# Regrouping an attention tile's TensorE work beside a two-layer expert network

## The chip, the cores and the metric

The kernel runs on one core of one Trainium2 chip. The metric is the device time of one launch in microseconds. TensorE does all matrix products; VectorE (DVE), ScalarE (ACT) and GpSimd (POOL) do the elementwise work; SyncE (SP) issues the DMAs. Each engine works through its own list of instructions in order and waits where an input is not ready.

## The reference, cut to what matters

An mLSTM with exponential gates (4 batch rows, 8 heads, 768 steps, head size 40), then two expert layers on 3072 tokens of width 320 with 2048 hidden units.

```python
for t in range(S):                                   # per batch row and head
    m_new = maximum(f[t] + m, i[t])
    f_stab, i_stab, m = exp(f[t] + m - m_new), exp(i[t] - m_new), m_new
    C = f_stab * C + i_stab * outer(v[t], k[t])      # 40 x 40 state
    n = f_stab * n + i_stab * k[t]
    y[t] = sigmoid(o[t]) * (C @ q[t]) / maximum(abs(n @ q[t]), 1.0)
x = y as [3072, 320]
x = square(maximum(x @ w_in, 0)) @ w_out             # first layer
h = x @ w2_in
out = (h * sigmoid(h)) @ w2_out                      # second layer
```

## The kernel before, in words

The recurrence is worked in chunks of 128 steps: 24 tiles of 128 tokens (`TILES`, a batch row and a chunk each; tiles 0 to 17 interleave three batch rows, 18 to 23 are the fourth). For one tile the steps are, by the names in the plan:

- `q`, `v`, `w`, `e`: loads; `sk`, `sj`: queries and keys split into float32r parts and stacked by DMA (`stk`); `m0`, `m1`, `x0`, `x1`: the decay weights W of the two halves of four heads.
- `s0`, `s1` (`SC`, L479): scores of heads 0 to 3 and 4 to 7, four products each, every half into a psum bank. `d0`, `d1` (`SD`): VectorE multiplies them by W and splits the result into three bf16 parts.
- `vk` (`VK`, L521): VectorE (in a few tiles GpSimd) scales the keys in place, for the state.
- `h` (`HG`, L547 and L558): head outputs, in groups of three, three and two heads. A group is one float32 product of the query with the state of the chunk before (L547, two instructions in the trace; none in the first chunk of a batch row), then six bf16 value products for each head (L558). Tiles 3 to 5 have float32 value products (L553) instead.
- `ev` (`EV`): VectorE divides and gates hA and makes y. `st` (`ST`, L585): the state products of the chunk, from vk, six instructions; none in the last chunk of a batch row. `gr`, `gm` (`GR`, `GM`): VectorE adds them into the state cc and masks it (in the first chunk ScalarE copies them out, L595 and L596).
- `xt` (`XT`, L618): three transposes of y. `xa`, `xl`: ScalarE and VectorE copy them out as the first layer's input x.

Scores, hA, state and transposes take their banks from one psum pool, `p_at`, with three banks.

The first layer runs in eight blocks of 384 tokens, three tiles each. In a block, a slot j of 16 has eight products for the hidden units three slots ahead (L677, `hin`) and eight for the output (L732 to L739, `o`). Tiles of the next blocks are worked between them: `base(i)` gives the slot at which tile i begins (16/3 slots per tile, six slots ahead), and `plan(i)` adds an offset for each step. Up to slot 16 (`KF`, block 0) a step's place comes from a written order with due times (`ORDER`); from there on steps are put into half slots by `at_slot` and issued by `run_events` in order of their time, first after the slot's `hin` products, then after its `o` products. In the blocks from the second to the last but one, TensorE, ScalarE, VectorE and SyncE keep exactly the order in which the program issues; in block 0 GpSimd does too. From the last block on only TensorE does. Tiles from 8 on begin at slot 16 or later, tile 7 at 15.33. The second layer (L749 to L751) has no attention beside it.

In steady state the steps of one tile on TensorE were so placed, in slots from its base b:

```python
("s0", b, ...), ("s1", b + 1.0, ...), ("vk", b + 2.6, VK),      # vk: VectorE
("h", b + 3.3, ...), ("ev", b + 3.9, EV), ("st", b + 4.4, ST),  # ev: VectorE
("xt", min(b + 6.1, e - 1.6), XT)                               # e: the block's due slot
```

The next tile's base is b + 5.33, so `xt` stood about 0.77 slot after the next tile's `s0`.

Of the kernel before, what the change touches and what calls it, by code (L numbers as in the profile page):

```python
# [18 lines left out]
PAIRS = ((2, 0), (1, 0), (1, 1), (0, 2), (0, 1), (0, 0))  # L19

B, H, S, D = 4, 8, 768, 40
# [3 lines left out]
NTILE = NT // L  # L25
KF = DFF // 128
# [11 lines left out]
N_EARLY = 3  # L38
# [76 lines left out]
def top(ap):  # L115
    return ap.bitcast(BF16).rearrange("p (n two) -> p n two", two=2)[:, :, 1]
# [3 lines left out]
def mlstm_moe_kernel(  # L120
# [14 lines left out]
    pe, act, dve, pool, sp = nc.tensor, nc.scalar, nc.vector, nc.gpsimd, nc.sync  # L135
# [185 lines left out]
    T = {}  # L321
# [135 lines left out]
    def sc_bank(i, hf):  # L457
        if i == 0:
            return p_in.tile([128, 512], F32, tag="in", name="sc")
        if i == 1:  # L460
            return p_out.tile([128, 512], F32, tag=f"o{1 + hf}", name="sc")
        return p_at.tile([128, 512], F32, tag="at", name="sc")

    def SC(i, hf):
        d = T[i]
        if i < N_NAT:
            if hf == 0:
                for p in range(2):
                    d["sc", p] = sc_bank(i, p)
                for h in range(4):  # L470
                    for p in range(2):
                        x = d["kq"][64 * p:64 * p + D]
                        pe.matmul(d["sc", p][:, h * L:(h + 1) * L], x[:, 0, h], x[:, 1, h], start=True, stop=True)
            return
        ps = d["sc", hf] = sc_bank(i, hf)
        for h in range(4):
            g, x = divmod(4 * hf + h, 3)
            gs = slice(g * L, (g + 1) * L)
            pe.matmul(ps[:, h * L:(h + 1) * L], d["stk"][0:120, x, 0, gs], d["stk"][0:120, x, 1, gs],  # L479
                      start=True, stop=True)  # L480

    def SD(i, hf):
        d = T[i]
        ps = d["sc", hf]
        w = d["W", hf]
        if i < N_EARLY:
            dve.tensor_tensor(out=w, in0=ps.rearrange("p (h t) -> p h t", h=4), in1=w, op=ALU.mult)
            d["p1", hf] = w.rearrange("p h t -> p (h t)")
            return
        if i < N_NAT:  # L490
            p = d["p1", hf] = at.tile([128, 4 * L], F32, tag="pr", name="pn", bufs=2)
            dve.tensor_tensor(out=p, in0=ps, in1=w.rearrange("p h t -> p (h t)"), op=ALU.mult)
            return
        dve.tensor_tensor(out=w, in0=ps.rearrange("p (h t) -> p h t", h=4), in1=w, op=ALU.mult)
        w = w.rearrange("p h t -> p (h t)")
        d["p1", hf] = top(w)
        r = at.tile([128, 4 * L], F32, tag="pr", name="pr", bufs=2)
        d["p2", hf] = top(r)
        p3 = d["p3", hf] = at.tile([128, 4 * L], BF16, tag="p3", name="p3", bufs=2)
        on(f"pr{hf}", i).tensor_tensor(out=r, in0=w, in1=d["p1", hf], op=ALU.subtract)  # L500
        on(f"p3{hf}", i).tensor_tensor(out=p3, in0=r, in1=d["p2", hf], op=ALU.subtract)
# [30 lines left out]
        q = d["q"][0:120].rearrange("p (g t) -> p g t", g=3)  # L532
        (pool if PLAN.get(f"@qt{i}", i < N_NAT) else dve).tensor_tensor(out=q, in0=q, in1=eqv(i)[0:120], op=ALU.mult)

    def HG(i, g):
        d = T[i]
        n = min(3, H - 3 * g)
        b, c = TILES[i]
        if g == 0 and i < N_EARLY:
            d["hA"] = p_out.tile([128, 512], F32, tag=f"o{i}", name="hA")  # L540
        elif g == 0:
            d["hA"] = p_at.tile([128, 512], F32, tag="at", name="hA")
        ov = d["hA"][:, 0:VW].rearrange("p (h c) -> p h c", c=42)
        if c:
            k = 40 * n
            q = d["q"][0:k, g * L:(g + 1) * L]
            pe.matmul(ov[:, 3 * g:3 * g + n], q, T["cm", b % 3][0:k, 3 * g:3 * g + n], start=True, stop=False)  # L547
        if i < N_NAT:
            v = d["vk"][:, DM:DM + VW].rearrange("p (h c) -> p h c", c=42)
            for h in (range(4 * g, 4 * g + 4) if i < N_EARLY else range(3 * g, 3 * g + n)):  # L550
                hf, k = place(i, h)
                p = d["p1", hf][:, k * L:(k + 1) * L]
                pe.matmul(ov[:, h], p, v[:, h], start=c == 0, stop=c == 0 or h == 3 * g + n - 1)  # L553
            return
        for h in range(3 * g, 3 * g + n):
            ps = [d[x, h // 4][:, (h % 4) * L:(h % 4 + 1) * L] for x in ("p1", "p2", "p3")]
            for m, (x, y) in enumerate(PAIRS):
                pe.matmul(ov[:, h], ps[x], d["v"][y][:, h], start=c == 0 and m == 0, stop=m == len(PAIRS) - 1 and (c == 0 or h == 3 * g + n - 1))  # L558

    def EV(i):  # L560
        d = T[i]
# [73 lines left out]
    i = 0  # L635
# [145 lines left out]
    if True:  # L781
# [29 lines left out]
        def base(i):  # L811
            if i < 2 * nb0:
                return 0.3 + 3.3 * (i - nb0)
            return KF * (i // 3 - 1) + KF * (i % 3) / 3 - EV_AHEAD

        def plan(i):
            b = base(i)
            p = base(i - 2) if i >= nb0 + 2 else -20.0
            e = KF * (i // 3) - AHEAD
            q0, v0, w0, e0 = b - 8.0, b - 5.0, b - 6.4, b - 4.6  # L820
            if i < nb0 + 2:
                q0, v0, w0, e0 = [(t - F0) / SLOT for t in LOADS[i - nb0]]
            else:
                q0, v0 = max(q0, p + (1.2 if i < N_NAT else 2.4)), max(v0, p + 4.8)
                w0, e0 = max(w0, p + 3.8), max(e0, p + 5.5)
            todo = [("q", q0, load_q), ("v", v0, load_v), ("w", w0, load_w), ("e", e0, load_e),
                    ("sk", max(b - 4.9, q0 + 0.6), SK), ("sj", max(b - 4.2, q0 + 1.2), SK2),
                    ("m0", b - 2.4, lambda i: WT(i, 0)), ("m1", b - 2.3, lambda i: WT(i, 1)),
                    ("x0", b - 1.8, lambda i: WE(i, 0)), ("x1", b - 1.2, lambda i: WE(i, 1)), ("vv", b - 1.5, VV),
                    ("s0", b, lambda i: SC(i, 0)), ("d0", b + 0.5, lambda i: SD(i, 0)), ("qt", b + 0.9, QT),  # L830
                    ("s1", b + 1.0, lambda i: SC(i, 1)), ("d1", b + 1.5, lambda i: SD(i, 1)),
                    ("vk", b + 2.6, VK),
                    ("h", b + 3.3, lambda i: (HG(i, 0), HG(i, 1), HG(i, 2))), ("ev", b + 3.9, EV),
                    ("st", b + 4.4, ST), ("gr", b + 4.9, GR), ("gm", b + 4.91, GM),
                    ("xt", min(b + 6.1, e - 1.6), XT), ("xa", min(b + 6.6, e - 1.1), XA),
                    ("xl", min(b + 6.9, e - 0.6), XL)]
            if i % 3 == 0:
                todo.append(("sg", b - 0.9, lambda i: load_s(i // 3)))
                todo.append(("si", b + 1.5, lambda i: sig(i // 3)))
            need = {"sk": "q", "sj": "sk", "m0": "w", "m1": "w", "x0": "m0", "x1": "m1", "s0": "q sj", "s1": "s0", "d0": "s0 x0",  # L840
                    "d1": "s1 x1", "qt": "q e", "vv": "v", "vk": "v", "h": "d0 d1 vv v qt", "ev": "h", "st": "vk vv v h", "gr": "st e",
                    "gm": "gr", "xt": "ev", "xa": "xt", "xl": "xa", "si": "sg", "e": "gd", "w": "gd", "x": "aw"}
            for nm, x, fn in todo:
                if x < KF or f"{nm}:{i}" in PLAN:
                    after = [f"{y}:{i}" for y in need.get(nm, "").split() if y not in ("gd",)]
                    if nm in ("w", "e"):
                        after += ["gD1", "eD1"]
                    if nm in ("m0", "x0", "vk"):
                        after += ["take"]
                    if nm in ("sk", "sj") and i < N_NAT:  # L850
                        continue
                    if nm == "h" and TILES[i][1]:
                        after.append(f"gm:{i - 3}")
                    if nm == "gr" and TILES[i][1]:
                        after += [f"gr:{i - 3}", f"h:{i}"]
                    if nm == "gm" and TILES[i][1]:
                        after += [f"h:{i}"]
                    if nm == "ev":
                        after.append(f"si:{i // 3 * 3}")
                    after = [y for y in after if y != f"sj:{i}" or i >= N_NAT]  # L860
                    GUESS[f"{nm}:{i}"] = F0 + SLOT * x
                    add(f"{nm}:{i}", lambda fn=fn: fn(i), *after)
                else:
                    at_slot(x, lambda fn=fn: fn(i))
# [21 lines left out]
        for k, (n, tag) in enumerate(WARM):  # L886
            n = int(PLAN.get(f"#warm{k}", n))
# [49 lines left out]
        for k, e in enumerate(wq):  # L937
            dec = []
            b = base(6 + k)
# [155 lines left out]
```

## Time and profile before

| | |
|---|---|
| median of 3 runs | 850.65 us (849.47 to 863.62) |
| profiled execution, its own time | 850.39 us |
| span of that execution in the trace | 848.7 us |
| TensorE busy | 824.7 us, 97% of the span |
| VectorE, ScalarE, GpSimd busy | 505.6, 492.5, 85.7 us |
| granted TensorE clock, mean | 0.994 |

The span runs from the first to the last instruction of the program on the core; 1.7 us of the time lie outside it. In the rows, L is a line of the kernel before; `out<-in` are the program's names; a form such as 120x126 is partitions x elements. The ends of matmuls are modelled and overlap the next one's start, so lengths of TensorE work are read from the chain of waits, where pieces follow one another without overlap.

### The profile page before, as it was taken

The numbers are of one execution on the slowest core, as the hardware profiler recorded it, in microseconds if no ns is written. First come the engines' busy times: TensorE is split into PE (matmuls) and PEld (weight loads), VectorE is DVE, ScalarE is ACT, GpSimd is POOL, SyncE is SP. The second block draws the span as 40 slices with busy tenths as digits, with TensorE's granted clock in tenths as the row PEclk, the third lists the DMA queues.
The fourth block names the chain that finished last, engine by engine and source line by source line (L and its number), as shares of the span: only waits on it lengthen the run. The fifth ranks groups of instructions, "written<-read, shape, count | busy, mean of one in ns | idle before, by whom it ended". The sixth has DMA issues, their size and how long they took to land.

```text
span 848.7 us, 14676 instructions
## 1 busy us (share of the span) xinstructions
PE 824.7 (97%) x5569; PEld 773.4 (91%) x5569; DVE 505.6 (60%) x905; ACT 492.5 (58%) x966; POOL 85.7 (10%) x110
## 2 busy tenths in 40 slices
PE   7888899999999999999999999999999999999998
PEld 5677889999999999999999999999999999999997
DVE  3789899888787787787742333353443433433433
ACT  3587787786976977869746553343433433433332
POOL 4244143100001000000000110000000000000000
PEclk9899999999999999999999999999999999999999
DMA  6667758767767676677403990020010000000000
GB/s 234 179 210 245 238 161 269 252 197 237 224 220 238 219 251 219 202 235 229 144 1 119 308 293 31 1 81 1 24 58 1 8 25 0 32 1 1 32 1 32
DMA packets 69014, 115.68 MB, mean 136 GB/s; under 512 B 5175, under 2 KB 47039, under 8 KB 68943
## 3 DMA queue, kind: packets, MB, share of 16 engines
q1 hardware_dynamic: 68943, 114.74, 42.8%
q8 instruction: 44, 0.72, 0.4%
q14 instruction: 27, 0.22, 0.1%
HBM read 75.48 MB, written 19.33 MB: 112 GB/s over the span
## 4 chain that ended last, share of the span: by engine, by line
PE 87%; DVE 2%; DMA 2%; ACT 1%; SPq 1%; issue 1%; POOL 1%; DVEq 0%; POOLq 0%; ACTq 0%
PE hin L677 40%; PE o L751 7%; PE o L750 7%; PE o L749 7%; PE o L732 5%; PE o L733 5%; PE o L734 5%; PE hA L558 3%; PE o L737 2%; PE o L739 2%; PE hA L547 2%; PE sc L479 2%; PE st L585 1%; DMA rqk<-in_qk_dram 1%; DMA W<-g_d 1%; DMA wo<-w2o_d 1%
## 5 line engine op out<-in xcount | busy, mean ns | idle before, releaser
L677 PE MATMUL hin<-x,wi 128*128 128x384 f32 (+1 forms) x1792 | 400.1, 365 | 5.9 <-ACT r L687 2.9
L677 PEld LDWEIGHTS hin<-x,wi 128*128 128x128 f32 x1792 | 321.7, 189 | 33.8 <-ACT r L687 3.7
L708 DVE TENSOR_TENSOR gl<-r,gh 128x384 fp32r<-128x384 f32 (+1 forms) x224 | 140.8, 631 | 112.4 <-ACT gh L694 60.7
L694 ACT ACTIVATE gh<-r 128x384 fp32r<-128x384 f32 (+1 forms) x224 | 127.8, 571 | 70.9 <-DVE r L690 65.4
L690 DVE TENSOR_TENSOR r<-hin,r 128x512 f32<-128x512 f32 x96 | 66.4, 691 | 136.4 <-ACT r L689 136.4
L689 ACT ACTIVATE r<-hin 128x512 f32<-128x512 f32 x96 | 57.3, 597 | 148.2 <-PE hin L677 148.2
L751 PE MATMUL o<-wo,gl 128*128 128x320 f32 x384 | 118.7, 309 | 0.0
L750 PE MATMUL o<-wo,gh 128*128 128x320 f32 x384 | 118.5, 309 | 0.0
L749 PE MATMUL o<-wo,gh 128*128 128x320 f32 x384 | 118.2, 308 | 0.0
L687 ACT ACTIVATE r<-hin 128x384 f32<-128x384 f32 x128 | 62.1, 487 | 84.0 <-PE hin L677 80.5
L732 PE MATMUL o<-gh,wo 128*128 128x384 f32 x256 | 89.6, 350 | 0.0
L734 PE MATMUL o<-gl,wo 128*128 128x384 f32 x256 | 86.7, 339 | 1.3 <-DVE gl L708 1.3
L733 PE MATMUL o<-gh,wo 128*128 128x384 f32 x256 | 86.8, 339 | 0.1
L749 PEld LDWEIGHTS o<-wo,gh 128*128 128x128 f32 x384 | 72.1, 188 | 3.6
L750 PEld LDWEIGHTS o<-wo,gh 128*128 128x128 f32 x384 | 72.1, 188 | 3.6
L751 PEld LDWEIGHTS o<-wo,gl 128*128 128x128 f32 x384 | 72.1, 188 | 0.0
L702 ACT ACTIVATE r<-r 128x384 f32<-128x384 f32 x123 | 64.6, 525 | 3.9
L444 POOL TENSOR_SCALAR_AFFINE_SELECT W<-W 128x512 f32<-128x512 f32 x42 | 32.8, 804 | 246.9 <-DMA W<-g_d 176.5
L455 ACT ACTIVATE W<-W,aw 128x128 f32<-128x128 f32 x168 | 52.9, 390 | 0.1
L734 PEld LDWEIGHTS o<-gl,wo 128*128 128x128 f32 x256 | 48.3, 189 | 1.7 <-DVE gl L708 1.7
L733 PEld LDWEIGHTS o<-gh,wo 128*128 128x128 f32 x256 | 48.4, 189 | 0.6 <-POOL wo L296 0.5
L732 PEld LDWEIGHTS o<-gh,wo 128*128 128x128 f32 x256 | 48.5, 189 | 0.4
(142 smaller groups left out, 1015.6 us busy)
## 6 DMA issues: line engine op xcount, KB each, us to landing
stk<-tt SPq DMA_DIRECT2D x162, 120.0 KB
raw<-in_w_in_dram SPq DMA_DIRECT2D x16, 768.0 KB
W<-g_d SPq DMA_DIRECT2D x21, 512.0 KB
raw<-in_w_out_dram SPq DMA_DIRECT2D x16, 640.0 KB
vk<-in_vk_dram SPq DMA_DIRECT2D x23, 328.0 KB
rqk<-in_qk_dram SPq DMA_DIRECT2D x18, 360.0 KB
w2i_d<-ws SPq DMA_DIRECT2D x8, 640.0 KB
w2o_d<-ws SPq DMA_DIRECT2D x8, 640.0 KB
```

Source lines behind the costliest of these rows:

```text
L677: pe.matmul(ps[:, 0:N], w[:, c, ws], x[:, sl, 0:N], start=(k == 0), stop=(k == 7))
L687: act.activation(out=r, in_=ps, func=ACTF.Relu)
L690: dve.tensor_tensor(out=r, in0=ps, in1=r, op=ALU.mult)
L694: act.activation(out=gh, in_=r, func=ACTF.Square if blocks[bi][0] == 1 else ACTF.Copy)
L702: act.activation(out=r, in_=r, func=ACTF.Square)
L708: on("gl" if ly == 1 else "gl2", gi).tensor_tensor(out=gl, in0=r, in1=f(gh), op=ALU.subtract)
L732: pe.matmul(o[k][:, 0:N], w[:, c], gh, start=first, stop=False)
L733: pe.matmul(o[k][:, 0:N], w[:, c2], gh, start=False, stop=False)
L734: pe.matmul(o[k][:, 0:N], w[:, c], gl, start=False, stop=last)
L749: pe.matmul(o[k][:, 0:DM], gh[:, c], w[:, 0:320], start=first, stop=False)
L750: pe.matmul(o[k][:, 0:DM], gh[:, c], w[:, 320:640], start=False, stop=False)
L751: pe.matmul(o[k][:, 0:DM], gl[:, c], w[:, 0:320], start=False, stop=last)
```

## The change

For tiles whose base is at slot 16 or later, `s1` moves from b + 1.0 to directly behind `s0`, and the transposes of tile i - 1 directly behind both (`nx` is the next tile's base; `xa` and `xl` follow at the same distances as before). `st` moves from b + 4.4 to directly in front of `h` wherever that place is at slot 16 or later, which takes in tile 7. The head outputs of every planned tile (3 to 23) run in two parts: all query-state products of the three groups, then all value products; the flags that open and close the accumulation in the bank are set for the whole bank instead of for a group. The other steps keep their offsets.

```diff
--- before.py
+++ after.py
@@ -532,30 +532,41 @@
         q = d["q"][0:120].rearrange("p (g t) -> p g t", g=3)
         (pool if PLAN.get(f"@qt{i}", i < N_NAT) else dve).tensor_tensor(out=q, in0=q, in1=eqv(i)[0:120], op=ALU.mult)
 
-    def HG(i, g):
+    def HG(i, g, part=3):
         d = T[i]
         n = min(3, H - 3 * g)
         b, c = TILES[i]
-        if g == 0 and i < N_EARLY:
+        if part == 2:
+            pass
+        elif g == 0 and i < N_EARLY:
             d["hA"] = p_out.tile([128, 512], F32, tag=f"o{i}", name="hA")
         elif g == 0:
             d["hA"] = p_at.tile([128, 512], F32, tag="at", name="hA")
         ov = d["hA"][:, 0:VW].rearrange("p (h c) -> p h c", c=42)
-        if c:
+        if c and part & 1:
             k = 40 * n
             q = d["q"][0:k, g * L:(g + 1) * L]
-            pe.matmul(ov[:, 3 * g:3 * g + n], q, T["cm", b % 3][0:k, 3 * g:3 * g + n], start=True, stop=False)
+            pe.matmul(ov[:, 3 * g:3 * g + n], q, T["cm", b % 3][0:k, 3 * g:3 * g + n],
+                      start=part == 3 or g == 0, stop=False)
+        if part == 1:
+            return
+        end = 3 * g + n - 1 if part == 3 else H - 1
         if i < N_NAT:
             v = d["vk"][:, DM:DM + VW].rearrange("p (h c) -> p h c", c=42)
             for h in (range(4 * g, 4 * g + 4) if i < N_EARLY else range(3 * g, 3 * g + n)):
                 hf, k = place(i, h)
                 p = d["p1", hf][:, k * L:(k + 1) * L]
-                pe.matmul(ov[:, h], p, v[:, h], start=c == 0, stop=c == 0 or h == 3 * g + n - 1)
+                pe.matmul(ov[:, h], p, v[:, h], start=c == 0, stop=c == 0 or h == end)
             return
         for h in range(3 * g, 3 * g + n):
             ps = [d[x, h // 4][:, (h % 4) * L:(h % 4 + 1) * L] for x in ("p1", "p2", "p3")]
             for m, (x, y) in enumerate(PAIRS):
-                pe.matmul(ov[:, h], ps[x], d["v"][y][:, h], start=c == 0 and m == 0, stop=m == len(PAIRS) - 1 and (c == 0 or h == 3 * g + n - 1))
+                pe.matmul(ov[:, h], ps[x], d["v"][y][:, h], start=c == 0 and m == 0, stop=m == len(PAIRS) - 1 and (c == 0 or h == end))
+
+    def HGA(i):
+        for part in (1, 2):
+            for g in range(3):
+                HG(i, g, part)
 
     def EV(i):
         d = T[i]
@@ -823,17 +834,20 @@
             else:
                 q0, v0 = max(q0, p + (1.2 if i < N_NAT else 2.4)), max(v0, p + 4.8)
                 w0, e0 = max(w0, p + 3.8), max(e0, p + 5.5)
+            s1 = b + 0.01 if b >= KF else b + 1.0
+            st = b + 3.29 if b + 3.29 >= KF else b + 4.4
+            nx = base(i + 1) if i + 1 < NTILE and base(i + 1) >= KF else 99.0 * KF
+            xt, xa, xl = [min(b + u, e - v, nx + w) for u, v, w in ((6.1, 1.6, 0.02), (6.6, 1.1, 0.52), (6.9, 0.6, 0.9))]
             todo = [("q", q0, load_q), ("v", v0, load_v), ("w", w0, load_w), ("e", e0, load_e),
                     ("sk", max(b - 4.9, q0 + 0.6), SK), ("sj", max(b - 4.2, q0 + 1.2), SK2),
                     ("m0", b - 2.4, lambda i: WT(i, 0)), ("m1", b - 2.3, lambda i: WT(i, 1)),
                     ("x0", b - 1.8, lambda i: WE(i, 0)), ("x1", b - 1.2, lambda i: WE(i, 1)), ("vv", b - 1.5, VV),
                     ("s0", b, lambda i: SC(i, 0)), ("d0", b + 0.5, lambda i: SD(i, 0)), ("qt", b + 0.9, QT),
-                    ("s1", b + 1.0, lambda i: SC(i, 1)), ("d1", b + 1.5, lambda i: SD(i, 1)),
+                    ("s1", s1, lambda i: SC(i, 1)), ("d1", b + 1.5, lambda i: SD(i, 1)),
                     ("vk", b + 2.6, VK),
-                    ("h", b + 3.3, lambda i: (HG(i, 0), HG(i, 1), HG(i, 2))), ("ev", b + 3.9, EV),
-                    ("st", b + 4.4, ST), ("gr", b + 4.9, GR), ("gm", b + 4.91, GM),
-                    ("xt", min(b + 6.1, e - 1.6), XT), ("xa", min(b + 6.6, e - 1.1), XA),
-                    ("xl", min(b + 6.9, e - 0.6), XL)]
+                    ("h", b + 3.3, HGA), ("ev", b + 3.9, EV),
+                    ("st", st, ST), ("gr", b + 4.9, GR), ("gm", b + 4.91, GM),
+                    ("xt", xt, XT), ("xa", xa, XA), ("xl", xl, XL)]
             if i % 3 == 0:
                 todo.append(("sg", b - 0.9, lambda i: load_s(i // 3)))
                 todo.append(("si", b + 1.5, lambda i: sig(i // 3)))
```

## Rows read from the trace of the kernel before

**Rows 1.** The page's part 1: busy us of each engine, share, instructions.

```profile
PE 824.7 (97%) x5569; PEld 773.4 (91%) x5569; DVE 505.6 (60%) x905; ACT 492.5 (58%) x966; POOL 85.7 (10%) x110
```

**Rows 2.** Two stretches: length, PE, PEld, DVE, ACT, POOL busy, TensorE's granted clock, DMA.

```profile
150.00:450.00 300.00, 300.00 (x2471) 295.19 (x2470) 227.52 (x457) 229.76 (x477) 21.75 (x29) 1.00 0.64 201
199.28:208.08 8.80, 8.80 (x55) 8.69 (x54) 8.54 (x13) 5.37 (x11) 1.68 (x2) 1.00 0.86 279
```

**Rows 3.** Chain of waits, tiles 12, 13: start of a piece, length, instructions.

```profile
228.08 0.22 PE hA L547 x2
228.30 0.45 PE hA L558 x18
228.75 0.31 PE hA L547 x2
...
229.51 0.28 PE hA L547 x2
229.78 0.30 PE hA L558 x12
230.09 0.27 PE o L732
230.35 0.18 PE o L733
...
232.99 0.58 PE st L585 x6
233.57 0.21 PE o L732
...
236.43 0.40 PE sc L479 x4
236.83 0.22 PE o L732
...
239.71 0.33 PE xT L618 x3
240.03 0.40 PE sc L479 x4
240.43 0.22 PE o L732
```

**Rows 4.** Timeline, VectorE: tile 7 (two rows), 9, 15, 19, 20.

```profile
131.16 2.66 DVE L501 TENSOR_TENSOR p<-pr 128x512 bf16<-128x512 f32 x2
...
134.74 0.48 DVE L521 TENSOR_TENSOR vk<-vk,aw 128x320 f32<-128x320 f32 x1
...
169.82 0.49 DVE L521 TENSOR_TENSOR vk<-vk,aw 128x320 f32<-128x320 f32 x1
...
291.32 0.20 DVE L573 COPY y<-y 128x64 f32<-128x64 f32 x1
...
358.42 0.48 DVE L521 TENSOR_TENSOR vk<-vk,aw 128x320 f32<-128x320 f32 x1
...
375.61 0.49 DVE L521 TENSOR_TENSOR vk<-vk,aw 128x320 f32<-128x320 f32 x1
```

**Rows 5.** Timeline, TensorE: head outputs 7, 9; scores 16, 19; head outputs 19, 20.

```profile
133.73 0.38 PE L547 MATMUL hA<-cm,rqk 120*128 120x126 f32 x2
...
171.13 0.27 PE L547 MATMUL hA<-cm,rqk 120*128 120x126 f32 x1
...
292.47 0.34 PE L479 MATMUL sc<-stk 120*128 120x128 f32 x2
...
347.36 0.34 PE L479 MATMUL sc<-stk 120*128 120x128 f32 x2
...
358.43 0.27 PE L547 MATMUL hA<-cm,rqk 120*128 120x126 f32 x1
...
376.39 0.27 PE L547 MATMUL hA<-cm,rqk 120*128 120x126 f32 x1
```

**Rows 6.** Timeline, ScalarE: the state of tile 18.

```profile
348.31 0.22 ACT L596 ACTIVATE cc<-st 80x84 f32<-80x84 f32 x1
```

## Prediction

> **What bounds the kernel now.** The page's first part comes first: TensorE is busy for 824.7 of 848.7 us, VectorE and ScalarE for some 60% [rows 1]. A mean hides stages, so the second view is busy time by stretch: from 150 to 450 us, where tiles 8 to 23 are worked beside blocks 1 to 6 of the first layer, TensorE has no idle time at all, at full granted clock [rows 2]. There every 10 ns that its queue saves is worth 10 ns, and every wait put into that queue costs its whole length. The third view is the chain of waits, read for the length of each TensorE piece: a plain block product takes 0.18 us, and what deviates from that is the price of a change between kinds of product [rows 3]. Last, since the change moves instructions ahead in an in-order queue, the timeline tells when what they need is ready [rows 4 to 6].
>
> **Head outputs: what grouping saves.** Before, a tile with an earlier state runs pair, 18 value products, pair, 18, pair, 12. (The pair is one float32 query-state product in two instructions; the value products are bf16.) The first pair, entered from a block product, takes 0.22 us; the second and third, entered from value products, 0.31 and 0.28 [rows 3]. With all six instructions in front, pairs 2 and 3 follow a pair: I price them at 0.22, so 0.09 + 0.06 = 0.15 us go. The value products keep 0.45 + 0.45 + 0.30 = 1.20 us, plus at most 0.02, and the long first block product behind them (0.27 against 0.18) stays. Bounds: 0.11 us (the first pair, now entered from the state product, takes 0.03 more, which is what the block product after a state pays: 0.21 against 0.18) to 0.18 us (that 0.03 is saved instead). I take 0.14 us, near the rows of the pair itself. Tiles 7 to 17 and 19 to 23, sixteen of them, gain: 16 x 0.14 = **2.24 us**, bounds 1.8 to 2.9. Tile 6 gains too, but loses it in tile 7's wait (below); tiles 3 to 5 have float32 value products, so no change of kind is removed; tile 18 starts a batch row, has no query-state product, and can save at most 0.03.
>
> Why a pair costs more behind value products: those are spaced 0.45/18 = 25 ns, too short to cover the next weight load. The Trainium skill, "TensorE: Matmul & The Clock Gate", in "Step-by-step: what each phase is for", says that the next tile's weights load while the present matmul runs. Taken without limit, that rule speaks against the change: the pair's weights would be loaded under the value products, and grouping would save nothing. The rows (0.31 and 0.28 against 0.22) disagree with it behind 25 ns products; the result by it is rival 4.
>
> **Scores and transposes: nothing, I think.** Four scores take 0.40 us and lengthen the next block product by 0.04 (0.22 against 0.18); the transposes take 0.33, and the piece behind them is not lengthened: scores straight behind transposes take the usual 0.40 and 0.04 [rows 3]. That neighbouring pair of runs already exists before and is worth nothing. In a run of eight, the four later scores no longer enter from a long product, so I price them at 0.44 and the total is unchanged: 0.44 + 0.44 + 0.33. Bounds: 0.04 saved (one exit less) to 0.03 lost per tile, over sixteen tiles +0.6 to -0.5 us; I take 0, by the row where the two kinds stand side by side. As for the work that fed the gaps: the block products between old and new places still have to run, only in another order.
>
> **What moves past what.** No DMA is moved; SyncE's and GpSimd's lists keep their order. On ScalarE and VectorE the two copies of the transposes (xa, xl) come 0.7 slot earlier, same work. On TensorE three things come earlier, each behind a producer:
> - The transposes move ahead by about 0.75 slot and need y. The tightest tile I found is 15: y ready at 291.32 + 0.20 = 291.52, the next tile's scores start at 292.47 and the transposes 0.88 later [rows 4, 5]: 1.8 us of margin. No wait.
> - The state products move from behind the head outputs to in front of them. They need vk, scaled on VectorE and issued only 0.7 slot before. In tile 7 VectorE is late: two subtractions alone take 2.66 us, and vk is ready at 134.74 + 0.48 = 135.22 [rows 4]. TensorE reaches the head outputs at 133.73 [rows 5]. Before, the state stood 4.9 us later and nothing waited; now it stands first, and head outputs, block products and all later tiles queue behind it. Cost against the old times: 135.22 - 133.73 = **1.49 us** (the wait itself is longer by tile 6's gain, which it swallows). VectorE is not waiting for TensorE here, so the time of vk does not move.
> - The second score half and the transposes take psum banks earlier. In the program of before, the three "at" banks are handed out in the order in which they come free; carried over, the transposes of tile 18 get the bank of tile 18's state, which ScalarE copies out as late as 348.31 + 0.22 = 348.53 [rows 6]. TensorE would be there at 347.36 + 0.88 = 348.24 [rows 5]: a wait of 0.3 us. It is not a sum of its own, because tile 19's vk is ready at 358.42 + 0.48 = 358.90 and the head outputs stood at 358.43 [rows 4, 5]: whatever came before, the state of tile 19 starts **0.47 us** later than the head outputs did. Bounds for this place: 0.47 (VectorE keeps its time) to 0.8 (the second scores, not the transposes, get that bank: 348.53 - 347.36 - 0.44 = 0.73).
> In the other tiles that write a state, vk is in time: eight have margins from 376.39 - 376.10 = 0.29 us (tile 20) to 171.13 - 170.31 = 0.82 (tile 9), two have more than 1.2 [rows 4, 5]; in tile 8 GpSimd scales it long before.
>
> **Sum**, against the profiled execution (848.7 us span, 850.39 us its time): -2.24 + 0 + 1.49 + 0.47 = -0.28, so **850.1 us**. That execution lies 0.26 under the median of the three runs, well within their own scatter (849.47 and 850.65 are the two close ones).
>
> **Rivals.**
> 1. The waits do not come (vk ready in time everywhere). All gains stand, tile 6's too: 850.39 - 2.24 - 0.14 = 848.0. Against it: VectorE's queue in tile 7 has no idle time to give back.
> 2. Each end of a run has a price of its own, so merging runs saves it: 0.04 for a score half, 0.03 for a state, sixteen tiles: 1.1 us more, 849.0. For it: the 0.22 and 0.21 us products [rows 3]. Against it: a run's first product is short by as much.
> 3. Slower: vk comes late in every tile. The bundle of scores and transposes delays the next block products by 0.78 us (0.44 + 0.33), ScalarE and VectorE get them later, and vk slips with them. It decides where vk has less than 0.78 of margin: eight tiles, mean margin 0.53, 8 x 0.25 = 2.0, and tile 19 in full, 0.78: 850.1 + 2.8 = 852.9. Against it: between scores and vk VectorE has no slack to wait in (8.54 of 8.80 us busy in tile 11 [rows 2]); it runs on its own backlog, so a later input need not move it.
> 4. The weight loads were hidden anyway: no gain, both waits stay: 850.39 + 1.49 + 0.47 = 852.4.
> That the change does not do what it says would be a bank or y that holds the new run apart; only tile 18 looks like it, and its price is in the sum.
>
> **How the numbers follow.** Forecast (849.2 to 851.0) 0.55; rival 1 0.17; rival 2 0.08; rival 3 0.12; rival 4 0.05; anything else 0.03 (in the last block and the second layer the framework orders ScalarE, VectorE and SyncE anew). The range reaches from rival 1 less the scores' bound to rival 3: 847.6 to 852.9. 2% of this kernel is 17 us, about what one can tell from no change; all terms together are a third of that, so faster and slower get 0.01 each.
>
> **What would show it.** Right: six query-state instructions in one piece of 0.66 to 0.70 us, 48 value products in one of 1.2, the state in front; a TensorE wait of some 1.6 us for vk in tile 7, one of 0.3 for the copy of tile 18's state, one of 0.1 to 0.2 for vk in tile 19; scores and transposes together still some 1.2 us. Wrong: waits for vk in tiles 10 to 14 (rival 3), none in tile 7 (rival 1), a piece of query-state products near 0.8 (rival 4), or TensorE waiting in the second layer, which I have not costed.

## The result, and the profile after

The changed kernel takes 860.37 us (median of 12 runs, 855.19 to 868.51), the kernel before 854.06 (12 runs beside it, 849.47 to 864.6). The ratio is 1.0076, 95% interval 1.0047 to 1.0105: slower by 4.0 to 9.0 us, where 0.3 us of gain was forecast. It is a small loss, below 2%, and a real one.

The part ahead of tile 6 differs by more than ten microseconds between executions of one and the same kernel (the first head outputs of tile 6 begin at 127.8 us in this profile of the changed kernel, at 115.8 in another), so spans of two profiles are not compared here. This profile is of a slow execution (868.51 us) and the other of a fast one (856.33): in their first 60 us TensorE's granted clock was 0.69 and 0.94, while in the stretch compared here it is 1.00 in this profile as in that of before. What is compared is **the stretch** from tile 6's first query-state product to tile 23's first transpose, which holds all but the start of the changed work: 325.15 us before (118.58 to 443.73), 331.31 after (127.83 to 459.14). Its +6.2 us is of the size of the loss that the runs show; the second profile gives +8.7 (below).

The page's first part, which answers to [rows 1], is no help: TensorE's busy share hardly moves.

```profile
PE 835.5 (96%) x5569; PEld 780.7 (90%) x5569; DVE 500.2 (58%) x905; ACT 491.9 (57%) x966; POOL 84.6 (10%) x110
```

Busy time by stretch does better (same columns as [rows 2]). Where TensorE never idled, it is now busy for 304.68 of 310 us; over the stretch it was busy for all 325.15 us and is now for 323.83 of 331.31, 7.5 us of idle time against 1.3 us of busy time saved. In tile 11, from its first score to the end of vk, VectorE is busy for 7.99 of 11.23 us, where it was busy for 8.54 of 9.23 (the row of before begins 0.43 us behind the score): it has been made to wait.

```profile
150.00:460.00 310.00, 304.68 (x2510) 298.81 (x2509) 230.36 (x472) 234.29 (x489) 23.64 (x33) 1.00 0.65 204
209.83:221.06 11.23, 9.80 (x60) 9.34 (x59) 7.99 (x15) 7.78 (x15) 1.59 (x2) 1.00 0.80 249
```

The table of waits names what TensorE waits for in the stretch (us in total, times, the longest). Before, it had no row. (Waits below 0.15 us have no row.)

```profile
PE st L596 <- DVE vk L521: 6.9, 4, 2.2
PE xT L629 <- ACT cc L607: 0.4, 1, 0.4
```

The chain of waits shows that the moved work itself is as forecast (start of the piece, length; lines are 11 higher behind the head outputs): eight scores in 0.85, three transposes in 0.35, the state in 0.58, six query-state instructions in 0.67, 48 value products in 1.21, and one long product (0.27) at the end. Before, the head outputs took 2.01 us without the state, and the state lengthened what followed it [rows 3].

```profile
153.54 0.85 PE sc L479 x8
154.38 0.35 PE xT L629 x3
...
163.18 0.58 PE st L596 x6
163.75 0.67 PE hA L549 x6
164.42 1.21 PE hA L564 x48
...
243.44 0.27 PE o L743
243.71 0.18 PE o L744
```

TensorE's timeline of the two kinds of loss: in tile 7 the state begins at 145.13 after 2.16 us idle, in tile 11 at 221.21 after 1.58, both ended by vk. In front of tile 11's wait stand the bundled scores and transposes and the next `hin` products.

```profile
145.13 0.34 PE L596 MATMUL st<-vk 128*120 128x126 f32 x1 [2.16 <-DVE vk L521]
...
209.83 1.01 PE L479 MATMUL sc<-stk 120*128 120x128 f32 x8
210.67 0.52 PE L629 MATMUL xT<-ident,y 128*128 128x128 f32 x3
210.94 0.42 PE L688 MATMUL hin<-x,wi 128*128 128x384 f32 x1
...
221.21 0.45 PE L596 MATMUL st<-vk 128*120 128x126 f32 x2 [1.58 <-DVE vk L521]
```

VectorE around the same places, vk of tile 7 first and then tile 11 from the split of the first half to vk (`x<-xT,x` is xl):

```profile
144.50 0.48 DVE L521 TENSOR_TENSOR vk<-vk,aw 128x320 f32<-128x320 f32 x1
...
212.65 0.69 DVE L501 TENSOR_TENSOR p<-pr 128x512 bf16<-128x512 f32 x1
215.78 0.56 DVE L643 TENSOR_TENSOR x<-xT,x 128x384 fp32r<-128x384 f32 x1 [2.44 <-ACT x L639]
...
220.58 0.48 DVE L521 TENSOR_TENSOR vk<-vk,aw 128x320 f32<-128x320 f32 x1
```

and ScalarE in tile 11:

```profile
212.62 0.49 ACT L698 ACTIVATE r<-hin 128x384 f32<-128x384 f32 x1 [1.92 <-DVE pr L500]
...
214.13 0.83 ACT L424 ACTIVATE tt<-rqk 120x768 fp32r<-120x768 f32 x1
214.86 0.51 ACT L425 ACTIVATE tt<-rqk 120x384 fp32r<-120x384 f32 x1
215.28 0.47 ACT L639 ACTIVATE x<-xT 128x384 fp32r<-128x384 f32 x1
```

For comparison tile 11 of before: its first score, then on VectorE the split of the second half (d1), xl and vk:

```profile
198.85 0.56 PE L479 MATMUL sc<-stk 120*128 120x128 f32 x4
...
206.05 0.69 DVE L501 TENSOR_TENSOR p<-pr 128x512 bf16<-128x512 f32 x1
206.66 0.55 DVE L632 TENSOR_TENSOR x<-xT,x 128x384 fp32r<-128x384 f32 x1
...
207.59 0.49 DVE L521 TENSOR_TENSOR vk<-vk,aw 128x320 f32<-128x320 f32 x1
```

This is the step to read. xl, VectorE's copy of the transposes, now stands in front of qt, tt and the second half's d1. VectorE reaches it at 213.34 and idles 2.44 us, until ScalarE's xa has run at 215.28. ScalarE could not run xa sooner: first comes the relu of the `hin` products that the bundle pushed back (they begin 1.11 us after the scores, 0.39 before), then two more steps of that block, then the splits for the next tile (0.83 and 0.51 us). (The relu's row names VectorE's `pr`, which ends within some hundredths of a microsecond of the last `hin` product; in tile 14 the same wait, 1.81 us, is ended by the `hin` products.) So vk, behind xl on VectorE, ends 221.06 - 209.83 = 11.23 us after the first score, where it took 208.08 - 198.85 = 9.23 before. TensorE, which before had 0.42 us to spare at this place, now stands in front of the state products and waits.

The same happens in tiles 11, 14 and 20, the last tile of a block each, where the half slots put xl ahead of qt and d1 and vk is on VectorE: from one tile's last value product to the next one's takes 19.63 us instead of 17.81 with vk in time (the kernel vk_early below), 3 x 1.82 = 5.5 us. Tile 7 loses 17.99 - 15.58 = 2.4. The other tiles lose 1.2 together. That is 9.1 us, against 2.9 gained: +6.2.

### The profile page after: what moved, and what is told of

Read it like the earlier page. It is cut to its first block, busy times and chain, and to the rows that moved or that the text cites. A ratio compares the mean times of both kernels' runs of the same rounds, so it can differ in the third digit from the quotient of the medians.

```text
span 866.8 us, 14686 instructions
## 1 busy us (share of the span) xinstructions
PE 835.5 (96%) x5569; PEld 780.7 (90%) x5569; DVE 500.2 (58%) x905; ACT 491.9 (57%) x966; POOL 84.6 (10%) x110
## 4 chain that ended last, share of the span: by engine, by line
PE 76%; DVE 6%; DMA 6%; ACT 3%; issue 2%; POOL 1%; SPq 1%; DVEq 0%; ACTq 0%; POOLq 0%
PE hin L688 36%; PE o L762 6%; PE o L761 6%; PE o L760 6%; PE o L743 4%; PE o L744 4%; PE o L745 4%; PE hA L564 2%; PE o L748 2%; PE o L750 2%; DMA vk<-in_vk_dram 2%; PE sc L479 1%; PE hA L549 1%; DMA xr<-x_d 1%; DVE gl L719 1%
## 5 line engine op out<-in xcount | busy, mean ns | idle before, releaser
L705 ACT ACTIVATE gh<-r 128x384 fp32r<-128x384 f32 (+1 forms) x224 | 127.8, 570 | 69.2 <-DVE r L701 65.4
```

The costliest lines, as they stand in the source:

```text
L705: act.activation(out=gh, in_=r, func=ACTF.Square if blocks[bi][0] == 1 else ACTF.Copy)
```

## The experiments

Theory A: the copies, put earlier, make VectorE wait; vk slips; the state, put in front, hands that to TensorE. Rival B: the bundle is enough, since it delays the block products. Rival C: the state in front is late everywhere by itself. Rival D: the new runs cost by themselves and the waits only show it. No kernel below leaves out or changes any of the computation. Each is the changed kernel with the edit shown; the ratio is against the kernel before, run on the same chip.

| kernel | the stretch, us | TensorE's waits in it, us | ratio, 95% interval |
|---|---|---|---|
| before | 325.15 | none | |
| after | 331.31 | vk 6.9, state copy 0.4 | 1.0076, 1.0047 to 1.0105 |
| after, again | 333.82 | vk 7.2, state copy 0.2 | 1.0054, 1.0015 to 1.0092 |
| group_only | 322.98 | none | 1.0013, 0.9966 to 1.0059 |
| copies_back | 329.63 | vk 3.1, input 0.6, state copy 0.3 | 0.9987, 0.9944 to 1.0031 |
| state_back | 322.81 | state copies 0.8 | 0.9949, 0.9901 to 0.9996 |
| no_bundle | 328.75 | vk 2.4, input 0.8 | 1.0035, 1.0005 to 1.0065 |
| vk_early | 322.20 | state copy 0.3 | 1.0109, 1.0064 to 1.0155 |
| tile7_back | 328.94 | vk 5.2, state copy 0.2 | 1.0048, 1.0008 to 1.0088 |
| xl_back | 328.36 | vk 3.0, input 1.0, state copy 0.3 | one run |
| vk_early_later | 322.22 | state copy 0.3 | 1.0004, 0.9960 to 1.0048 |
| bundle_only | 325.03 | state copy 0.2 | 0.9955, 0.9916 to 0.9995 |

The stretch tells kernels apart to some tenths of a microsecond, the ratio, which carries the scatter of the start, only to some 4 us. Counting only executions with a mean granted clock of 0.983 or more, the mean time differs from that of before by +6.6 us (after, again), -1.5 (group_only), +2.4 (copies_back), -1.8 (state_back), +2.0 (no_bundle), +3.8 (tile7_back), -2.0 (vk_early_later) and -2.3 (bundle_only), each uncertain by 1.2 to 2.0 us. The signs are those of the stretch, and the sizes differ from it by up to 2.2 us.

**The changed kernel again.** No edit.

> The changed kernel once more, for a profile beside the others. Measure: from the first query-state product of tile 6 to the first transpose of tile 23, 325.15 us in the profile of before and 331.31 in that of after. Theory A (the copies xa and xl, put 0.7 slot earlier, make VectorE wait for ScalarE, vk slips by 2 us, and TensorE waits for vk in front of the state): 331.3 again, waits for vk of 1.6 to 2.2 us in tiles 7, 11, 14 and 20, and the first part of the kernel, ahead of tile 6, as before (about 119 us). Rival (the profiled run was a disturbed one, its waits come from late loads): fewer waits, 327 or less.

Measured: 333.82 us, the same waits in tiles 7, 11, 14 and 20 (2.42, 1.58, 1.58, 1.58). The rival falls; the waits are the kernel's. The extra 2.5 us, which A had not expected, has a cause of its own. Busy time by stretch of this second profile, the wait of tile 7 in the first row, what follows it in the second:

```profile
128.00:133.30 5.30, 2.96 (x17) 2.59 (x15) 5.30 (x8) 3.43 (x7) 3.30 (x3) 0.97 0.79 291
133.30:138.60 5.30, 5.22 (x63) 5.25 (x64) 4.01 (x10) 1.61 (x5) 0.00 (x0) 0.50 0.76 260
```

and the same two places in the first profile of after:

```profile
142.60:145.10 2.50, 0.37 (x3) 0.04 (x2) 2.50 (x5) 0.86 (x2) 1.57 (x2) 1.00 0.69 232
145.10:150.00 4.90, 4.87 (x73) 4.90 (x74) 3.61 (x9) 2.70 (x7) 0.00 (x0) 1.00 0.70 226
```

After the wait the granted clock is 0.50, the lower of the two levels (1.2 GHz), for more than 5 us of busy TensorE; in the first profile it stays at 1.00 behind a wait of 2.16 us. From tile 6's last value product to tile 8's takes 38.72 us instead of 35.81. So a wait of this size sometimes costs about twice its length. The Trainium skill, "TensorE: Matmul & The Clock Gate", in "What's actually happening", says that the throttled clock is the default and that activity releases it. This profile agrees: the clock fell behind idle time and rose again while TensorE was busy. The idle time's length alone does not tell which way it goes: behind waits of 2.13 us (copies_back) and 2.04 us (no_bundle) the clock fell, behind 2.16 us (here) and 2.00 us (xl_back) it did not.

**group_only.** Scores, state, transposes and copies as before:

```diff
-            s1 = b + 0.01 if b >= KF else b + 1.0
-            st = b + 3.29 if b + 3.29 >= KF else b + 4.4
-            nx = ...
-            xt, xa, xl = [min(b + u, e - v, nx + w) for u, v, w in ...]
+            s1, st = b + 1.0, b + 4.4
+            xt, xa, xl = [min(b + u, e - v) for u, v in ((6.1, 1.6), (6.6, 1.1), (6.9, 0.6))]
```

> Only the grouping of the head outputs; scores, state, transposes and copies stand as in the kernel before. Theory A: no wait on TensorE in the stretch, 0.15 to 0.17 us saved in each of 17 tiles (6 to 17, 19 to 23): 325.15 - 2.7 = 322.5 us, ratio 0.997. Rival (the grouping saves nothing, weight loads were hidden): 325.1 us, ratio 1.000.

Measured: 322.98, no wait in the table, 0.5 us over A's number. 2.17 us are saved in 17 tiles, 0.13 each on the mean. From one tile's last value product to the next one's, fourteen of the sixteen tiles 7 to 17 and 19 to 23 are 0.14 to 0.19 us shorter; tile 12 is 0.08 longer (the `hin` products in front of its head outputs take 1.65 us instead of 1.42) and tile 18, which has no query-state products, 0.30. The rival (weights hidden) falls. The ratio cannot see it.

**copies_back.** Only the transposes stay early:

```diff
-            xt, xa, xl = [min(b + u, e - v, nx + w) for u, v, w in ...]
+            xt, xa, xl = min(b + 6.1, e - 1.6, nx + 0.02), min(b + 6.6, e - 1.1), min(b + 6.9, e - 0.6)
```

> The changed kernel with the copies of the transposes, xa and xl, at their old places; the transposes themselves stay bundled and the state stays in front. Theory A: VectorE no longer idles some 2.4 us for xl, vk is in time in tiles 11, 14 and 20; waits are left in tile 7 (1.5 to 2.2 us) and 19 (0.5 or less): about 325 us, ratio 1.000. Rival B (the bundle on TensorE delays the block products, so vk is late whatever the copies do): waits for vk of 0.3 to 1.7 us in tiles 11, 14 and 20 stay, 328 us or more.

Measured: 329.63. By the letter this is rival B's result, 328 or more with waits of 0.3 to 1.7 us left in tiles 11, 14 and 20, and A's 325 was missed by 4.6 us. But half of what is lost against vk_early (below), 3.7 of 7.4 us, lies in tiles 7 and 8, where the wait of 2.13 us is followed by a lower granted clock:

```profile
146.50:152.00 5.50, 5.50 (x70) 5.50 (x71) 4.13 (x11) 1.37 (x5) 0.73 (x1) 0.69 0.80 256
```

TensorE's waits:

```profile
PE st L596 <- DVE vk L521: 3.1, 4, 2.1
PE hin L688 <- DVE x L643: 0.6, 2, 0.4
PE xT L629 <- ACT cc L607: 0.3, 1, 0.3
```

In tiles 11, 14 and 20 the wait falls from 1.58 to 0.33 us: most of it was the copies, as A says, but not all. VectorE in tile 11, xl without idle time in front of it, then vk:

```profile
221.31 0.55 DVE L643 TENSOR_TENSOR x<-xT,x 128x384 fp32r<-128x384 f32 x1
...
222.24 0.48 DVE L521 TENSOR_TENSOR vk<-vk,aw 128x320 f32<-128x320 f32 x1
```

vk ends 222.72 - 212.75 = 9.97 us after the first score, 0.74 later than before: that is B, by the size that the prediction's rival 3 gave it (0.78). Both are at work; A is the larger. With xl late again, the first layer's input comes late too (0.6 us in two places).

**xl_back.** xa stays early:

```diff
-            xt, xa, xl = [min(b + u, e - v, nx + w) for u, v, w in ...]
+            xt, xa, xl = min(b + 6.1, e - 1.6, nx + 0.02), min(b + 6.6, e - 1.1, nx + 0.52), min(b + 6.9, e - 0.6)
```

> The changed kernel with only xl, VectorE's copy, at its old place; ScalarE's xa stays early. Theory A' (it is VectorE's in-order wait at xl, not ScalarE's load, that makes vk late): the idle of 2.4 us before xl goes, waits for vk in tiles 11, 14 and 20 fall from 1.6 to 0.3 to 0.5 us, as with both copies back. Rival (xa in front of ScalarE's other work delays the chain): the waits stay above 1 us.

Measured: 328.36, and 0.33 us in tiles 11, 14 and 20, as with both copies back. It is VectorE's place in its own queue, not ScalarE's.

```profile
PE st L596 <- DVE vk L521: 3.0, 4, 2.0
```

**state_back.**

```diff
-            st = b + 3.29 if b + 3.29 >= KF else b + 4.4
+            st = b + 4.4
```

> The changed kernel with the state products at their old place behind the head outputs; scores, transposes and copies stay moved. Theory A: VectorE still idles 2.4 us for xl, but nothing on TensorE needs vk early; the head outputs of tiles 11, 14, 17, 20 and 23 may wait 0.1 to 0.3 us for the third bf16 part: 323 to 324 us, ratio 0.998. Rival B (the bundle costs by itself): 326 us or more.

Measured: 322.81; 2.34 us saved, with bundle and early copies in place. VectorE still idles 2.9 us for xl in tile 11, and nobody waits for it. Rival B falls as a cause that acts alone: but for the two short waits below, the bundle costs nothing unless the state stands in front. This is a version that beats both kernels in the stretch, ratio 0.9949. Its waits are for copies of a state, which hold a bank:

```profile
PE xT L629 <- ACT cc L607: 0.6, 1, 0.6
PE xT L629 <- DVE cc L612: 0.2, 1, 0.2
```

**no_bundle.** The state alone in front, with the grouping:

```diff
-            s1 = b + 0.01 if b >= KF else b + 1.0
+            s1 = b + 1.0
...
-            xt, xa, xl = [min(b + u, e - v, nx + w) for u, v, w in ...]
+            xt, xa, xl = [min(b + u, e - v) for u, v in ((6.1, 1.6), (6.6, 1.1), (6.9, 0.6))]
```

> The changed kernel with second scores, transposes and copies at their old places; grouped head outputs and the state in front of them stay. The stretch (tile 6's first query-state product to tile 23's first transpose) is 325.15 us before, 331.3 to 333.8 after, 323.0 with the grouping alone. Theory A (copies and bundle together make vk late): waits for vk only in tile 7 (1.5 to 1.7 us, plus up to 2 us if the granted clock falls after it) and tile 19 (0.5): 325 us, 327 with the clock. Rival C (the state in front is late everywhere, with or without the bundle): waits for vk of more than 1 us in tiles 11, 14 and 20 too, 329 us or more.

Measured: 328.75, 1.7 us over A's number with the lower clock (it was 0.68 for 5.3 us behind the wait of tile 7) and just under C's 329. The waits for vk are in tiles 7 (2.04) and 19 (0.32) alone, as A had it, and none in 11, 14 and 20. So C falls by the place of the waits, not by the number. What I had not costed are three waits for the input, 0.2 to 0.35 us.

```profile
PE st L596 <- DVE vk L521: 2.4, 2, 2.0
PE hin L688 <- DVE x L643: 0.8, 3, 0.3
```

**tile7_back.**

```diff
-            st = b + 3.29 if b + 3.29 >= KF else b + 4.4
+            st = b + 3.29 if b >= KF else b + 4.4
```

> The changed kernel with the state behind the head outputs in tile 7 alone. Theory A: the 2.2 to 2.4 us wait there goes, and with it the stretch of granted clock 0.50 that followed it in one run; the waits of 1.6 us in tiles 11, 14 and 20 stay: 331.3 - 2.4 = 328.9 us. Rival (tile 7's wait is late loads or late VectorE that reappears elsewhere): 331 us or more, or a wait of 2 us in tile 8 or 9.

Measured: 328.94, as A had it to 0.1 us; what is left is four waits, 1.58 each in tiles 11, 14 and 20 and 0.4 in tile 21.

```profile
PE st L596 <- DVE vk L521: 5.2, 4, 1.6
```

**vk_early.**

```diff
-                    ("vk", b + 2.6, VK),
+                    ("vk", b + 0.85, VK),
```

> The changed kernel with nothing undone, but vk issued 1.75 slots earlier on VectorE, in front of xl and of the second half's split. Theory A (vk late in front of the state is the whole loss): no wait for vk in any tile, though VectorE still idles 2.4 us for xl; a wait of up to 0.6 us for tile 18's state copy stays, and some 0.1 to 0.3 us for the third bf16 part in tiles 11, 14, 17, 20 and 23: 323 us, ratio 0.996 to 0.998. Rival D (the bundle and the state run themselves cost, the waits only show it): 327 us or more.

Measured: 322.20 in the stretch, 0.8 under A's number, and no wait for vk. So vk was the whole loss in the stretch, and D falls. But the kernel is slower, 1.0109, where A had 0.996 to 0.998, with a wait that I brought in ahead of the stretch: in tile 7 the early vk stands in front of its own load on VectorE,

```profile
123.86 0.70 DVE L521 TENSOR_TENSOR vk<-vk,aw 128x320 f32<-128x320 f32 x1 [2.70 <-DMA vk<-in_vk_dram]
```

and the first layer's input behind it comes late (1.2 us of this wait stands in the kernel before as well):

```profile
128.16 0.69 PE L688 MATMUL hin<-x,wi 128*128 128x384 f32 x1 [5.24 <-DVE x L643]
```

Behind it the granted clock is 0.50 from 128.2 to 132 us, so more than the 4.0 us of added idle time is lost. That this is all of the 1.0109 is not shown; the next kernel takes the wait out.

**vk_early_later.** So tile 7 is left alone:

```diff
-                    ("vk", b + 2.6, VK),
+                    ("vk", b + (0.85 if b >= KF else 2.6), VK),
-            st = b + 3.29 if b + 3.29 >= KF else b + 4.4
+            st = b + 3.29 if b >= KF else b + 4.4
```

> The changed kernel with vk issued early (b + 0.85 slots) in tiles 8 to 23 alone, and tile 7 left as in the kernel before (vk at b + 2.6, state behind the head outputs), so that vk of tile 7 no longer waits for its load in front of block 1's input. Theory A (a state in front of the head outputs costs nothing where vk is in time): no wait for vk, the 5.2 us wait for the input that the early vk of tile 7 caused gone (1.2 us, as in every run, stays); stretch 322 to 322.6 us, ratio 0.995 to 0.998. Rival (early vk costs again elsewhere on VectorE): new waits on TensorE of more than 1 us in tiles 8 to 23, stretch 324 or more.

Measured: 322.22, and one wait on TensorE:

```profile
PE xT L629 <- ACT cc L607: 0.3, 1, 0.3
```

In tile 11 vk now runs before the idle time in front of xl, which is still 2.03 us and harmless:

```profile
204.67 0.48 DVE L521 TENSOR_TENSOR vk<-vk,aw 128x320 f32<-128x320 f32 x1
207.18 0.56 DVE L643 TENSOR_TENSOR x<-xT,x 128x384 fp32r<-128x384 f32 x1 [2.03 <-ACT x L639]
```

The stretch is 2.9 us below that of before, all of the change kept. The ratio (1.0004, where A had 0.995 to 0.998) does not tell it from no change; the stretch does, and so do the executions with a mean granted clock of 0.983 or more: 850.3 us on the mean (7) against 852.3 before (17), 2.0 us less, give or take 1.2.

**bundle_only.**

```diff
-            st = b + 3.29 if b + 3.29 >= KF else b + 4.4
+            st = b + 4.4
-                    ("h", b + 3.3, HGA),
+                    ("h", b + 3.3, lambda i: (HG(i, 0), HG(i, 1), HG(i, 2))),
```

> Only the bundle of scores and transposes with the copies moved; head outputs group by group, state behind them. By the price in the prediction (a run of eight costs as much as two of four, bounds 0.04 saved to 0.03 lost per tile): stretch 324.5 to 325.7 us, against 325.15 before, with a wait of 0.2 to 0.6 us for tile 18's state copy in it. Rival (each end of a run has its own price, 0.04 to 0.07 a tile, as rival 2 had it): 324.0 to 324.5 with that wait. Rival B (the bundle delays the block products and costs by itself): 326 or more.

Measured: 325.03, 0.12 under before, with the wait of 0.2 us for tile 18's state copy in it. Eight scores and three transposes take 0.84 + 0.35 us, and the products behind them their usual 1.39:

```profile
209.41 0.84 PE sc L479 x8
210.25 0.35 PE xT L629 x3
210.60 1.39 PE hin L688 x8
```

The sum is as priced, and rival B falls for the bundle alone. The price is not nothing, though. From one tile's last value product to the next one's, tiles 9, 10, 12, 13, 15, 16, 21 and 22 are 0.05 to 0.07 us shorter than before, the last tiles of a block (11, 14, 17, 20, 23) 0.01 and tile 18 0.15. State_back is shorter than group_only by 0.05 to 0.06 in tiles 9, 10, 13, 15, 16 and 22 and by 0.01 in the last tiles of a block. Tile 8 (0.21 longer) and tile 19 (0.35, 0.21 of it the wait for the state copy) give it back. In state_back those two tiles have the waits for a bank, so the cause is probably the same here; in tile 8 of this kernel no wait of that kind is seen. So rival 2's 0.04 for a score half has about the right size in two tiles of three and is hidden in the sum. The ratio, 0.9955, promises more than the stretch shows; why stays open.

## Why the prediction was wrong

The step that failed is the one on "What moves past what": "On ScalarE and VectorE the two copies of the transposes (xa, xl) come 0.7 slot earlier, same work", and, resting on it, "In the other tiles that write a state, vk is in time". I costed a moved instruction by its length and not by what it waits for at its new place. The prediction's own instruction order held the answer: xl needs xa, xa stands on ScalarE behind the relu of a block and the next tile's splits, and xl was moved past qt and d1 to where xa cannot yet be done. VectorE works in order, so the 2.44 us are paid by all behind it, vk among them. In tiles 11, 14 and 20 that put 5.5 us into the sum where it had nothing.

A second point concerns the base. The forecast counted from one execution of 850.39 us and its range ended at 852.9, but the median of twelve executions of the kernel before is 854.06; so 3.7 of the 10.3 us between 850.1 and 860.37 are the base and not the change.

- **Head outputs**: 0.14 a tile forecast, 0.14 to 0.19 measured where nothing else disturbs a tile, 0.13 on the mean (group_only). Right, if a little low.
- **Scores and transposes**: 0 forecast, 0.12 us in all measured (bundle_only). The sum is right by luck: 0.05 to 0.07 us saved in two tiles of three, and two tiles that give it back. Of rival 2 the score half holds there; its 0.03 for a state does not show (tiles 9 to 14 of vk_early_later differ from those of state_back by -0.01 to +0.03 us).
- **Weight loads (rival 4)**: out. The query-state piece is 0.67 us as forecast (0.66 to 0.70), not 0.8.
- **Tile 7**: the mechanism was right, the size off: 1.49 us forecast, 2.4 measured, and in the second profile, where the clock fell, 2.9 more in tiles 7 and 8 (0.3 of it a longer wait). vk came 144.98 - 133.16 = 11.82 us after the tile's first score instead of 135.22 - 124.10 = 11.12. That 0.7 is not the change's doing, as far as the runs show: with the grouping alone, which moves nothing of VectorE's, it is 11.80, in the second profile of after 12.07, in tile7_back 10.88. VectorE's slow steps there (2.67 us for two subtractions, as before) are the same; in front of them it waited 0.80 us for a split of ScalarE, 0.25 before, and that split had waited 1.12 us for its load, 0.60 before. So the time of vk in tile 7, read from one execution, is uncertain to about a microsecond, and with it the forecast wait. A further 0.15 us, from the end of vk to the first state product (145.13 - 144.98), was left out of every margin.
- **Tile 18**: 0.3 us forecast for the bank, 0.4 and 0.2 of idle time measured in the two profiles. Right. But the term in the sum was tile 19's wait for vk, 0.47 us, and that did not come with the bundle: TensorE reaches this state at 372.65 and vk is ready at 372.10. That the place costs about the sum's 0.47 is luck.
- **Tiles 11, 14, 20**: margins of 0.29 to 0.42 were forecast to hold; 1.58 us of idle time each, 5.5 in the stretch. Rival 3 named the place and the direction, with 0.78 us of slip where 2.0 were measured: its 0.78 is the bundle's share, as copies_back shows, and the copies add the rest. My argument against it ("VectorE has no slack to wait in") was taken from the trace of before, where xl stood behind d1; it said nothing on the new order. (Its 0.44 + 0.33 is 0.77, and 848.0 less 0.6 is 847.4, not 847.6; neither changes anything.)

As a gain the sum was 2.24 - 1.49 - 0.47; measured in the stretch it is 2.9 - 2.4 - 5.5 - 1.2.

## What to carry to other kernels

When an instruction is moved ahead in an in-order queue, ask what it waits for at the new place, on every engine where it was moved: an early consumer of a late producer holds everything behind it, and the loss shows on another engine. A margin read from the trace of before holds only while the order in front of it stays; once it is thinner than what you move, treat it as gone. Where one part of a change gains and another loses, take the stretch apart: here the grouping alone, or everything with the state left behind, keeps the gain, and moving vk ahead as well, in the tiles where its load has landed, keeps all of it. And a forecast of less than one per cent needs a base of more than one execution.

## What the runs showed of the hardware

- A wait of 2.42 us on TensorE was followed by more than 5 us at a granted clock of 0.50 and cost about 2.7 us beyond itself; behind waits of 2.13 and 2.04 us the mean granted clock was 0.69 and 0.68 for 5.5 and 5.3 us, behind waits of 2.16 and 2.00 us it stayed at 1.00.
- A pair of float32 products behind bf16 products that are 25 ns apart costs 0.06 to 0.09 us more than behind its own kind or a block product (0.31 and 0.28 against 0.22); three pairs in one piece take 0.67 us instead of 0.81.
- Putting two runs of four scores and the transposes together saves 0.05 to 0.07 us in two tiles of three and 0.01 in the third; putting the state products in front of the head outputs saves nothing that shows (-0.01 to +0.03 us).
